# v through a staging buffer, a cast and SBUF copies of key windows, in a sliding-window attention with a feed-forward layer

## The chip, the cores and the metric

The kernel runs on one core of a Trainium2 chip. Times are device microseconds (us) of that core. "The time of a kernel" is the median of its runs; a comparison is a ratio, computed as the mean time of one kernel's fast runs over that of the other's fast runs of the same rounds, with a 95% interval. It is therefore not quite the ratio of the medians that are quoted beside it. A run that is over 1.5% slower than the fastest of the same kernel counts as slow and stays out of the ratio.

## The reference, cut to what matters

```python
# q, k, v: [8 batches, 8 heads, 576 positions, 64]
scores = q @ k.T / sqrt(64);  mask = |i - j| <= 32
x = (softmax(where(mask, scores, -1e9)) @ v)        # -> [4608 tokens, 512]
h = x @ w_in                                        # [4608, 2048]
out = elu(h) @ w_out                                # [4608, 512]
```

All inputs and the output are fp32 in HBM. The kernel computes in bf16.

## The kernel before

Attention works on blocks of 64 queries. A block needs the 128 keys around it, so v lies in SBUF as nine *windows* per batch, `vw[key in window, window, head, 64 + 1]`: 128 partitions, a row of 520 bf16 (1040 bytes) per key and window, with a column of ones that yields the softmax sum. Two blocks make a *pair* (128 tokens; 36 pairs). Four pairs make a *tile* (in before the first tile is cut into two of two pairs), for which the hidden layer (matmul with w_in, ELU) and the output layer are computed while the next tile's pairs go through attention.

```python
NVB = 3                                   # three sets of windows
def load_v(b):                            # even windows, cast by the DMA itself: runs of 64 elements
    vt = vw[b % NVB]; vb = v[b].rearrange("h s d -> s h d")
    nc.gpsimd.dma_start(out=vt[WIN:128, 0, :, 0:D], in_=vb[0:128 - WIN])
    for qb in range(2, NQB - 1, 2):
        nc.gpsimd.dma_start(out=vt[:, qb, :, 0:D], in_=vb[lo:lo + 128])
    ...
def shift_v(b):                           # odd windows: two copies on the SP queue
    nc.sync.dma_start(out=vt[0:QB, 1:NQB:2], in_=vt[QB:128, 0:NQB - 1:2])
    nc.sync.dma_start(out=vt[QB:128, 1:NQB:2], in_=vt[0:QB, 2:NQB:2])
def X(i): nc.sync.dma_start_transpose(dst, xs)     # xt <- xs, on the SP queue too
def OUT(t, c): nc.sync.dma_start(out[r:r + 128, :], y)
```

q and k come as fp32 in four loads per batch, issued by ACT from batch 1 on, into four staging buffers `stg`; POOL casts them to `bf`. A planner in the kernel puts all operations in an order by assumed durations; on the chip each engine then works in that fixed order. In the built programs the transfers issued by SP or ACT take eight completion semaphores in turn: all 116 of before do, and all 192 of after. The records of the two traces show the same eight, and in them no transfer is issued before the one that used its semaphore before, eight places earlier in the program, has landed, whichever of the two engines issued that one. In after 13 are issued within 0.02 to 0.18 us of that landing; the two waits examined below are among them. I call this *the line of eight*. The transfers issued by POOL have semaphores of their own in the traces, eight in before (48 transfers) and four in after (4).

The softmax here doesn't subtract the row's maximum and nothing guards it: scores larger than these inputs give would overflow.

Of the kernel before, what the change touches and what calls it, by code (L numbers as in the profile page):

```python
# [8 lines left out]
FP32 = mybir.dt.float32  # L9
BF16 = mybir.dt.bfloat16  # L10
AX = mybir.ActivationFunctionType
ALU = mybir.AluOpType
# [8 lines left out]
class Plan:  # L21
# [5 lines left out]

    def __init__(self):
        self.ops = {}

    def op(self, name, eng, dur, rank, deps, fn, dma=0.0, lag=0.0,
           at=0.0):


        self.ops[name] = (eng, dur, rank, tuple(deps), fn, dma, lag, at)

    def run(self):
        ops = self.ops
        done, users, left = {}, {}, {}
        for n, o in ops.items():  # L40
            left[n] = len(o[3])
            for d in o[3]:
                assert d in ops, (n, d)
                users.setdefault(d, []).append(n)
        free = {}
        server = 2.0
        ready = {}
        for n, o in ops.items():
            free.setdefault(o[0], 0.0)
            if left[n] == 0:  # L50
                ready.setdefault(o[0], {})[n] = 0.0
        order = []
        while len(order) < len(ops):
            best = None
            for e, rs in ready.items():
                if not rs:
                    continue
                t = max(free[e], min(rs.values()))
                n = min((ops[n][2], n) for n, r in rs.items() if r <= t)[1]
                if best is None or t < best[0]:  # L60
                    best = (t, e, n)
            t, e, n = best
            del ready[e][n]
            _, dur, _, _, fn, dma, lag, at = ops[n]
            free[e] = t + dur
            if dma:
                server = max(server, t + dur) + dma
                end = server + 2.0
            else:
                end = t + dur + lag  # L70
            end = max(end, at)
            done[n] = end
            order.append((t, n))
            for u in users.get(n, ()):
                left[u] -= 1
                if left[u] == 0:
                    ue = ops[u][0]
                    r = max(done[d] + (0.0 if ops[d][0] == ue
                                       and not (ops[d][5] or ops[d][6] or ops[d][7]) else self.LAT)
                            for d in ops[u][3])  # L80
                    ready.setdefault(ue, {})[u] = r
        self.done = done
        self.order = order
        for _, n in order:
            ops[n][4]()
# [3 lines left out]
def kernel(  # L89
# [47 lines left out]
    w_in_sb = const.tile([128, NDO, D_FF], BF16)  # L137
    w_out_sb = const.tile([128, NFO, DM], BF16)
    NKB = 2
    NVB = 3  # L140
    NPB = 2
    kT = [const.tile([128, HP, KW], BF16, name=f"kT{i}") for i in range(NKB)]
    qT = [const.tile([128, HP, S], BF16, name=f"qT{i}") for i in range(NKB)]
    vw = [const.tile([128, NQB, H, VW], BF16, name=f"vw{i}") for i in range(NVB)]
    pm = [const.tile([128, H, 3 * QB], BF16, name=f"pm{i}") for i in range(NPB)]

    live = {}
# [47 lines left out]
            nc.vector.tensor_copy(dst, src)  # L195


    def load_v(b):
        vt = vw[b % NVB]
        vb = v[b].rearrange("h s d -> s h d")  # L200
        nc.gpsimd.dma_start(out=vt[WIN:128, 0, :, 0:D], in_=vb[0:128 - WIN])
        for qb in range(2, NQB - 1, 2):
            lo = qb * QB - WIN
            nc.gpsimd.dma_start(out=vt[:, qb, :, 0:D], in_=vb[lo:lo + 128])  # L204
        lo = (NQB - 1) * QB - WIN
        nc.gpsimd.dma_start(out=vt[0:S - lo, NQB - 1, :, 0:D], in_=vb[lo:S])  # L206

    def shift_v(b):
        vt = vw[b % NVB]
        nc.sync.dma_start(out=vt[0:QB, 1:NQB:2], in_=vt[QB:128, 0:NQB - 1:2])  # L210
        nc.sync.dma_start(out=vt[QB:128, 1:NQB:2], in_=vt[0:QB, 2:NQB:2])


    def QK(i):
# [73 lines left out]

    def XE(i):
        dst, pt = live.pop(("XT", i))  # L290
        nc.vector.tensor_copy(dst, pt)


    gs, es, ys = {}, {}, {}
# [12 lines left out]
    def EX(t, fo):  # L307
# [2 lines left out]
        nc.scalar.activation(e, ps, AX.Exp)  # L310
        es[t, fo] = (ps, e)

    def FF(t, fo):
        ps, e = es[t, fo]
        f = ep.tile([128, ps.shape[1]], BF16, name="f", tag="f")
        nc.vector.tensor_scalar(f, e, -1.0, 0.0, ALU.add, ALU.min)  # L316
        es[t, fo] = (ps, f)

    def GG(t, fo):
        ps, f = es.pop((t, fo))  # L320
        nc.vector.tensor_tensor(gs[t][:, fo, :], ps, f, ALU.max)  # L321

    def ypool(t, c):
        if t < NT - 1:
# [21 lines left out]
        nc.sync.dma_start(out[r:r + 128, :], ys.pop((t, c)))  # L346


    sizes = [2, 2] + [4] * 8
    tiles, where = [], {}  # L350
    p0 = 0
    for t, n in enumerate(sizes):
# [10 lines left out]
    w_in_v = moe_w_in.rearrange("(o p) f -> p o f", p=128)  # L363
    w_out_v = moe_w_out.rearrange("(o p) f -> p o f", p=128)

    def WI(c):
        nc.gpsimd.dma_start(out=w_in_sb[:, :, c * FC:(c + 1) * FC],
                            in_=w_in_v[:, :, c * FC:(c + 1) * FC])

    def WO(c):  # L370
        o = NFO // NWC
# [7 lines left out]
    def prank(i):  # L379
# [3 lines left out]
              ("k", 1): "POOL"}  # L383
    engs = {"DVE": nc.vector, "ACT": nc.scalar, "POOL": nc.gpsimd}
    cdur = {"DVE": 1.2, "ACT": 1.5, "POOL": 1.5}
    LAND = {(0, "k", 0): 6.2, (0, "q", 0): 8.2, (0, "k", 1): 10.5,
            (0, "q", 1): 13.0, (1, "k", 0): 27.0, (1, "q", 0): 31.0,
            (1, "k", 1): 35.0, (1, "q", 1): 39.0}
    for b in range(B):
        need = prank(b * NQB // 2)  # L390
        r0 = need - 60
        t0 = where[b * NQB // 2][0]
        early = [("H", max(t0 - 2, 0), 15 if t0 == 2 else 8)] if b > 1 else []
        for half in range(2):
            for nm in ("q", "k"):
                deps = list(early)
                if b == 1:
                    deps.append(("SM", 0))
                if b:
                    deps.append(("C", b - 1, nm, half))  # L400
                P.op(("L", b, nm, half), "ACT" if b else "SP", 0.1,
                     r0 + half, deps,
                     lambda b=b, nm=nm, half=half: load_qk(
                         b, nm, half, nc.scalar if b else nc.sync),
                     dma=0.0 if b < 2 else 2.2, lag=2.0,
                     at=LAND.get((b, nm, half), 0.0))
                eng = casts0[nm, half] if b == 0 else "POOL"
                deps = [("L", b, nm, half)]
                if b >= 2:
                    deps += [("T", b - 2, nm, hp) for hp in range(HP)]  # L410
                P.op(("C", b, nm, half), eng, cdur[eng], need - 30 + half, deps,
                     lambda b=b, nm=nm, half=half, eng=eng:
                     cast(b, nm, half, engs[eng]))
        deps = list(early)
        if b > 1:
            deps += [("WO", c) for c in range(NWC)]
        if b >= NVB:
            last = ((b - NVB + 1) * NQB - 1) // 2
            deps = [("AV", last, 0), ("AV", last, 1)]
        if b == 1:  # L420
            deps.append(("C", 0, "k", 1))
        P.op(("LV", b), "POOL", 4.5, (-2000, -899)[b] if b < 2 else r0, deps, lambda b=b: load_v(b),
             dma=5.0 if b > 1 else 0.0, at=(17.0, 45.0)[b] if b < 2 else 0.0)
        P.op(("SV", b), "SP", 0.2, need - 20, [("LV", b)],
             lambda b=b: shift_v(b), lag=4.5)
        for hp in range(HP):
            for nm in ("q", "k"):
                n = hp * 2 + (nm == "k")
# [13 lines left out]
                     lambda b=b, nm=nm, hp=hp: E(b, nm, hp))  # L442

    for c in range(NWC):
        P.op(("WI", c), "POOL", 1.0, -990 + c,
             [("C", 0, "k", 1)], lambda c=c: WI(c),
             at=(19.5, 24.0, 28.5, 33.0)[c])
        P.op(("WO", c), "POOL", 1.0, -890 + c, [("C", 1, "q", 1)],
             lambda c=c: WO(c),
             at=(50.0, 54.0, 58.0, 62.0)[c])  # L450

    for i in range(NPAIR):
        r = prank(i)
# [13 lines left out]
        P.op(("MK", i), "DVE", 0.85, r, deps, lambda i=i: MK(i))  # L467
        t, c = where[i]
        for g in range(2):
            deps = [("MK", i)] + [("SV", b) for b in bs]  # L470
            if i < NC0:
                if i:
                    deps.append(("RN", i - 1, g))
# [14 lines left out]
        if i < NC0:  # L488
            if i:
                deps.append(("X", i - 1))  # L490
            P.op(("XT", i), "PE", 0.3, r + 3, deps, lambda i=i: X(i))
            P.op(("X", i), "DVE", 0.42, r + 3, [("XT", i)],
                 lambda i=i: XE(i))
        else:
            P.op(("X", i), "SP", 1.2, r + 3, deps, lambda i=i: X(i), lag=4.0)

    hseq = [(t, fo) for t in range(NT) for fo in range(NFO)]
    for n, (t, fo) in enumerate(hseq):
        np_ = tiles[t][1]
        fr = np_ / 4  # L500
        r = PER * tiles[t][0] + 2 * fo * fr
        deps = [("X", tiles[t][0] + np_ - 1), ("WI", fo * NWC // NFO)]
        if n >= 3:
            deps.append(("GG",) + hseq[n - 3])
        if t >= 2:
# [4 lines left out]
        if n >= 3:  # L510
            deps.append(("FF",) + hseq[n - 3])
        P.op(("EX", t, fo), "ACT", 0.17 + 0.43 * fr, r, deps,
             lambda t=t, fo=fo: EX(t, fo))
        P.op(("FF", t, fo), "DVE", 0.1 + 0.33 * fr, r, [("EX", t, fo)],
             lambda t=t, fo=fo: FF(t, fo))
        P.op(("GG", t, fo), "DVE", 0.16 + 0.53 * fr, r, [("FF", t, fo)],
             lambda t=t, fo=fo: GG(t, fo))
# [23 lines left out]
    with tc.manual_schedule():  # L541
# [17 lines left out]
            channel_multiplier=-1)  # L559
        nc.gpsimd.tensor_copy(masks, mf)  # L560
        for t in vw:
            nc.vector.memset(t[0:WIN, 0, :, 0:D], 0.0)
            nc.vector.memset(t[128 - WIN:128, NQB - 1, :, 0:D], 0.0)
            nc.vector.memset(t[:, 0:NQB:2, :, D:VW], 1.0)
        for t in kT:
            nc.vector.memset(t[:, :, 0:WIN], 0.0)
            nc.vector.memset(t[:, :, WIN + S:KW], 0.0)
        for t in pm:
            nc.vector.memset(t[:, :, QB:2 * QB], 0.0)
        P.run()  # L570
# [30 lines left out]
```

## Time and profile before

| | before |
|---|---|
| time | 367.35 us (three runs, 365.93 to 369.72) |
| profiled span | 364.8 us, granted clock 0.991 |
| PE busy | 314.2 us (86%) |
| transfers on SP and ACT / on POOL | 116 / 48 |
| DMA time by queue, sum of shares | 78.3% of 364.8 us = 286 us of all 16 engines |

PE is the engine that should set the time. It stands still for 50.6 us, most of them in the first 130. The lines that show this are in the prediction.

### The profile page before, as it was taken

How to read it: one execution, taken by the hardware profiler on the slowest of the kernel's cores; microseconds unless marked ns; L12 is line 12 of the kernel's file. 1: busy time of each engine (PE TensorE's matmuls, PEld its weight loads, DVE VectorE, ACT ScalarE, POOL GpSimd, SP SyncE). 2: the span in 40 equal slices, each digit the busy share in tenths (PEclk: the TensorE clock that was granted, in tenths of full speed). 3: DMA queues.
4: the chain of work that ended last, by engine and by line, in shares of the span. 5: the costliest groups of instructions: out<-in, count | busy, mean ns of one | idle time of the engine just before them, and what ended most of it. 6: DMA issues, size and time to landing. Idle time of an engine off the chain costs nothing.

```text
span 364.8 us, 7010 instructions
## 1 busy us (share of the span) xinstructions
PE 314.2 (86%) x2725; PEld 168.9 (46%) x2768; DVE 252.9 (69%) x565; ACT 177.2 (49%) x290; POOL 86.1 (24%) x93
## 2 busy tenths in 40 slices
PE   1415889669877999999999999989999999999995
PEld 1314666334434544554455445445554444444442
DVE  4216899475779499886887787778788778756610
ACT  3431477236453654754565466555654535443421
POOL 7623810490036004500540240033000000000000
PEclk9999999899999899999999999999999999999999
DMA  8999999999698639994995793195112121111012
GB/s 173 172 251 276 121 198 194 196 135 174 147 242 102 72 101 214 131 138 105 242 127 69 175 210 85 45 234 114 45 51 66 46 58 45 43 49 40 29 65 78
DMA packets 81504, 46.13 MB, mean 126 GB/s; under 512 B 56384, under 2 KB 76864, under 8 KB 81472
## 3 DMA queue, kind: packets, MB, share of 16 engines
q0 software_dynamic: 41728, 8.92, 33.4%
q1 hardware_dynamic: 28544, 20.26, 25.4%
q10 hardware_dynamic: 11200, 16.52, 19.0%
q8 instruction: 21, 0.34, 0.4%
q14 instruction: 11, 0.09, 0.1%
HBM read 36.70 MB, written 9.44 MB: 126 GB/s over the span
## 4 chain that ended last, share of the span: by engine, by line
PE 58%; DVE 18%; DMA 14%; issue 3%; ACTq 2%; POOL 2%; ACT 1%; SPq 1%; POOLq 0%; DVEq 0%
PE psY L335 24%; PE psH L302 24%; DMA vw<-vw 6%; DVE g L321 6%; DVE f L316 6%; DMA xt<-xs 5%; DVE pm L243 4%; PE psO L255 4%; DMA vw<-in_v_dram 3%; PE psT L180 2%; DVE xs L270 2%; ACTq L155 2%; PE psS L220 2%; PE psO L335 1%; PE psS L335 1%
## 5 line engine op out<-in xcount | busy, mean ns | idle before, releaser
L302 PE MATMUL psH<-xt,w_in_sb 128*128 128x512 bf16 (+1 forms) x624 | 147.3, 360 | 4.5 <-DVE g L321 2.4
L310 ACT ACTIVATE e<-psH 128x512 f32<-128x512 f32 (+1 forms) x160 | 88.1, 555 | 115.9 <-PE psH L302 90.1
L335 PE MATMUL psY<-w_out_sb,g 128*128 128x512 bf16 x501 | 131.8, 383 | 3.1 <-ACT y L341 1.1
L316 DVE TENSOR_SCALAR f<-e 128x512 bf16<-128x512 f32 (+1 forms) x160 | 75.7, 473 | 45.8 <-ACT e L310 45.7
L321 DVE TENSOR_TENSOR g<-psH,f 128x512 bf16<-128x512 f32 (+1 forms) x160 | 102.0, 637 | 5.1
L302 PEld LDWEIGHTS <-w_in_sb 128*128 128x128 bf16 x640 | 60.4, 99 | 61.2 <-issue 6.1
L335 PEld LDWEIGHTS <-g 128*128 128x128 bf16 x576 | 52.3, 98 | 55.0 <-issue 2.7
L170 POOL CAST bf<-stg 96x1536 bf16<-96x1536 f32 x29 | 43.5, 1501 | 107.1 <-DMA stg<-in_k_dram 89.1
L255 PE MATMUL psO<-vw,pm 128*128 128x65 bf16 x544 | 30.7, 198 | 17.9 <-DMA vw<-vw 8.3
L231 ACT ACTIVATE pu<-psS 128x1024 bf16<-128x1024 f32 x36 | 36.8, 1021 | 12.7 <-PE psS L220 10.3
L255 PEld LDWEIGHTS <-pm 128*128 128x128 bf16 x576 | 27.1, 102 | 30.9 <-issue 8.1
L243 DVE TENSOR_TENSOR pm<-pu,masks 128x512 bf16<-128x512 bf16 x72 | 34.0, 514 | 4.8 <-ACT pu L231 4.8
L180 PEld LDWEIGHTS <-bf 96*128 96x128 bf16 x384 | 23.7, 104 | 28.2 <-ACT bf L168 8.1
L270 DVE TENSOR_TENSOR xs<-psO,rc 128x256 bf16<-128x256 f32 x68 | 28.9, 424 | 5.5 <-DMA xt<-xs 3.2
L180 PE MATMUL psT<-ident,bf 96*128 96x96 bf16 x348 | 25.4, 211 | 7.0 <-POOL bf L170 3.6
L341 ACT COPY y<-psY 128x512 f32<-128x512 f32 x33 | 19.4, 586 | 19.4 <-PE psY L335 14.3
L268 DVE RECIPROCAL rc<-psO 128x4 f32<-128x4 f32 x68 | 12.1, 178 | 22.0 <-PE psO L255 21.5
L193 ACT COPY qT<-psT 128x576 bf16<-128x576 bf16 x30 | 19.1, 638 | 15.9 <-PE psT L180 15.9
L204 POOL DMA_DIRECT2D vw<-in_v_dram x24 | 21.3, 900 | 15.5 <-PE psO L255 15.3
L220 PE MATMUL psS<-qT,kT 64*128 64x64 bf16 x576 | 16.0, 196 | 3.6 <-ACT pu L231 3.2
L220 PEld LDWEIGHTS <-kT 64*128 64x128 bf16 x576 | 11.3, 98 | 15.3 <-issue 14.5
L206 POOL DMA_DIRECT2D vw<-in_v_dram x8 | 6.5, 812 | 41.4 <-PE psO L255 40.6
(42 smaller groups left out, 74.1 us busy)
## 6 DMA issues: line engine op xcount, KB each, us to landing
out_dram<-y SPq DMA_DIRECT2D x36, 256.0 KB, 2.1
stg<-in_k_dram ACTq DMA_DIRECT2D x14, 576.0 KB, 9.3
stg<-in_q_dram ACTq DMA_DIRECT2D x14, 576.0 KB, 10.9
vw<-vw SPq DMA_DIRECT2D x16, 260.0 KB, 8.5
vw<-in_v_dram POOLq DMA_DIRECT2D x24, 128.0 KB, 8.2
w_in_sb<-in_moe_w_in_dram POOLq DMA_DIRECT2D x4, 512.0 KB, 13.7
w_out_sb<-in_moe_w_out_dram POOLq DMA_DIRECT2D x4, 512.0 KB, 11.3
vw<-in_v_dram POOLq DMA_DIRECT2D x16, 96.0 KB, 11.4
```

The lines of the kernel that those rows point to most:

```text
L170: eng.tensor_copy(dst, src)
L180: nc.tensor.transpose(pt[:, j, :], src[:, j, 2 * hp:2 * hp + 2, :], ident[0:PR, 0:PR])
L220: nc.tensor.matmul(psS[:, h % 2, s, hp, :], lhsT=kT[b % NKB][base:base + 64, hp, qb * QB:qb * QB + 128], rhs=qT[b % NKB][base:base + 64, h ...
L231: nc.scalar.activation(pu, live.pop(("S", i)), AX.Exp, scale=SCALE)
L243: nc.vector.tensor_mul(dst, pu[:, :, s], mb)
L255: nc.tensor.matmul(o[:, j, :], lhsT=p[:, h, s * QB:s * QB + 128], rhs=vw[b % NVB][:, qb, h, :], start=(s == 0), stop=(s == 1))
L270: nc.vector.tensor_mul(live["X", i][:, g * HP:(g + 1) * HP, :], o[:, :, 0:D], rb)
L302: nc.tensor.matmul(ps, lhsT=w_in_sb[:, do, fo * 128:(fo + 1) * 128], rhs=xts[t][:, do, :], start=(do == 0), stop=(do == NDO - 1))
L310: nc.scalar.activation(e, ps, AX.Exp)
L316: nc.vector.tensor_scalar(f, e, -1.0, 0.0, ALU.add, ALU.min)
L321: nc.vector.tensor_tensor(gs[t][:, fo, :], ps, f, ALU.max)
L335: nc.tensor.matmul(ps, lhsT=gs[t][:, fo, c * 128:(c + 1) * 128], rhs=w_out_sb[:, fo, :], start=(fo == 0), stop=(fo == NFO - 1))
```

## The change

The intent: v comes in long runs by hardware queues in place of 36,864 runs of 64 elements issued by POOL, is cast by POOL and then copied on chip into the windows. w_in likewise comes as fp32 and is cast on chip. All tiles get four pairs, and ACT takes some of the work of DVE in the first two tiles.

```diff
-    NVB = 3
+    NVB = 2
+    vbf = const.tile([VP, VT, H, VW], BF16)          # VP = 72 partitions, VT = 8 keys in each
-    def load_v(b): ...                                # 5 DMAs on POOL per batch
-    def shift_v(b): ...                               # 2 copies on SP per batch
+    def load_v(b, half, eng):                         # 2 loads per batch, ACT's queue from batch 1 on
+        t = stg.tile([VP, HP, VT * D], FP32, name="stg", tag="stg")
+        eng.dma_start(out=t, in_=v[b, half * HP:(half + 1) * HP].rearrange(
+            "h (p t) d -> p h (t d)", t=VT))          # runs of 2 KB
+    def cast_v(b, half, eng): ...                     # vbf <- stg
+    def window(b, qb):                                # 9 copies on SP per batch
+        nc.sync.dma_start(
+            out=vw[b % NVB][r:r + hi - lo, qb].rearrange("k h d -> k (h d)"),
+            in_=vbf[lo // VT:hi // VT].rearrange("p t h d -> p t (h d)"))
     ...
-        nc.vector.tensor_copy(dst, pt)                # xt of the first four pairs
+        nc.scalar.copy(dst, pt)
+            nc.scalar.activation(f, e, AX.Relu, bias=1.0, scale=-1.0)   # every 2nd block, tiles 0 and 1
-    sizes = [2, 2] + [4] * 8
+    sizes = [4] * 9
-    def WI(c): nc.gpsimd.dma_start(out=w_in_sb[...], in_=w_in_v[...])
+    def WL(c): nc.scalar.dma_start(out=wst[n][:, c % 2], in_=w_in_v[...])   # fp32, into g's buffers
+    def WI(c, half): ...                              # casts on POOL and ACT
     ...
```

A window copy reads 128 rows of 1040 bytes from 16 partitions, eight rows in each, and writes them to 128 partitions. With it there are 192 transfers (72 of them window copies) and 4 on POOL.

## The prediction

> **What bounds the kernel now.** I read the page's slices first, then the chain of waits, then windows of 10 us, then the PE timeline for the moments at which work starts.
>
> ```profile
> PE   1415889669877999999999999989999999999995
> DVE  4216899475779499886887787778788778756610
> PEclk9999999899999899999999999999999999999999
> DMA  8999999999698639994995793195112121111012
> GB/s 173 172 251 276 121 198 194 196 135 174 147 242 102 72 101 214 131 138 105 242 127 69 175 210 85 45 234 114 45 51 66 46 58 45 43 49 40 29 65 78
> ```
>
> A slice is 9.12 us. From slice 14 on (about 130 us) PE is full; before that it has holes, and DMA is at 9 tenths in the first ten slices while it moves only 121 to 276 GB/s. So there are two stages: to about 85 us the transfers set the pace, afterwards PE does. The windows of 10 us say how much is lost: up to 130 us PE is busy 89.6 us, so 40.4 us idle; from 130 to 364.8 only about 10 us idle.
>
> ```profile
> 7.39 11.70 DMA vw<-in_v_dram
> 19.10 10.88 DMA vw<-vw
> ...
> 60.58 13.35 DMA xt<-xs
> ...
> 84.68 9.62 DMA vw<-vw
> ```
>
> The chain names the early waits: v's first load ends at 19 us, its shifted copy at 30 us, and only then can the first probability-times-v product (AV) start. Later xt (a transpose by DMA) and the second shifted copy take 13 and 10 us each, far over the 4.3 us that the issue table has as the median of such a transpose: they stand in a full DMA system.
>
> ```profile
> q0 software_dynamic: 41728, 8.92, 33.4%
> q10 hardware_dynamic: 11200, 16.52, 19.0%
> ...
> stg<-in_k_dram ACTq DMA_DIRECT2D x14, 576.0 KB, 9.3
> vw<-vw SPq DMA_DIRECT2D x16, 260.0 KB, 8.5
> w_in_sb<-in_moe_w_in_dram POOLq DMA_DIRECT2D x4, 512.0 KB, 13.7
> w_out_sb<-in_moe_w_out_dram POOLq DMA_DIRECT2D x4, 512.0 KB, 11.3
> ```
>
> The GpSimd queue takes a third of the DMA time with 41,728 packets. 36,864 of them (8 batches x 576 rows x 8 heads) are v in runs of 64 elements.
>
> ```profile
> L302 PE MATMUL psH<-xt,w_in_sb 128*128 128x512 bf16 x496 | 127.0, 379 | 2.6 <-DVE g L321 1.4 <-DMA xt<-xs 0.4
> L302 PE MATMUL psH<-xt,w_in_sb 128*128 128x256 bf16 x128 | 20.3, 287 | 1.8 <-DVE g L321 1.1
> L170 POOL CAST bf<-stg 96x1536 bf16<-96x1536 f32 x29 | 43.5, 1501 | 107.1 <-DMA stg<-in_k_dram 89.1 <-DMA stg<-in_q_dram 18.0
> L204 POOL DMA_DIRECT2D vw<-in_v_dram x24 | 21.3, 900 | 15.5 <-PE psO L255 15.3
> ```
>
> [...] the cost in a full stream comes from the chain, where a group of four 512-wide ones takes 0.86 us, and of four 256-wide ones 0.60 us. There 8 AV take 0.24 us, 16 scores (QK) 0.34, 6 input transposes 0.26.
>
> ```profile
> 36.12 1.86 PE L302 MATMUL psH<-xt,w_in_sb 128*128 128x256 bf16 x8
> 83.76 1.89 PE L302 MATMUL psH<-xt,w_in_sb 128*128 128x512 bf16 x8
> ```
>
> These are the two marks that I use: the first hidden-layer matmul (36.1 us), and the first of pairs 4 to 7 (83.8 us), from which on it is a PE-bound stream. (A pair is 128 tokens; there are 36.)
>
> [...] the DMA view of the first 60 us shows 208 to 226 GB/s while v's short runs are in flight and 266 to 296 GB/s around 22 to 34 us, when w_in's 2 KB runs flow. [...] the 96x1536 cast takes 1501 ns on POOL and 1471 on ACT.
>
> **The change, part by part.**
>
> v: 40 loads issued by POOL (24 at 0.90 us, 16 at 0.81: 34 us) and 16 shifted copies go. In comes, per batch, two loads of 288 packets of 2 KB, two POOL casts of 2048 elements (1501 x 2048/1536 = 2.0 us each, an estimate by size), and nine copies of 1040-byte rows on the SP queue. POOL stays far from a bound: 15 such casts add 30 us and the DMA issues that go were 34 us, on an engine busy 24%. In DMA time 4608 short packets per batch become 576 + 1088 larger ones. q10's line gives 0.19 x 364.8 x 16/11200 = 99 ns for a packet of about 1.5 KB[...]. I do not count this as fewer busy DMA microseconds, but as a rate nearer to the 280 GB/s of long runs.
>
> Start: at 280 GB/s batch 0 (3.54 MB) is in by 2.5 + 12.6 = 15 us. Cast of the second half on DVE 1.3 us, two copies issued at 0.65 and some 3 us to land: first AV about 21 to 22 us, against 30.1 now. Then four pairs at the present step of about 2.3 us per pair (AV starts at 30.12 and 31.58, then DVE-bound): the first tile is complete at 31 to 32 us, if w_in (4.19 MB behind batch 0, 15 us more, so 30 us, and a cast of 1 us) is there too. The first hidden matmul comes at about 32, with four pairs ready and not two.
>
> w_in by HWDGE and cast on chip: 8 casts of 1024 elements at 1.0 us, four on POOL and four on ACT, early and beside transfers. No time of its own.
>
> One tile size: 32 groups of 256-wide matmuls at 0.60 become 16 at 0.86: 19.2 - 13.8 = 5.4 us of PE saved, inside a stage that does not run PE-bound, so it does not come out as such.
>
> ACT takes a Relu for every second block of the first two tiles, and the xt copies. In tile 0 ACT then has 16 exps (0.60), 8 Relus (about 0.60), 7 evacuations (0.64) and 7 load issues (about 0.6): 23 us, against DVE's 8 x 0.50 + 16 x 0.69 = 15 us. So tile 0 is ACT-bound, 32 to about 54 us; DVE, which was at 90 to 95% between 40 and 60 us, is relieved.
>
> The hinge is the start of tile 1's hidden layer, mark two. In the built order there lie between the end of tile 0 and that mark on PE: 13 groups of the output layer (11.2 us), 8 input transposes (2.1), 7 QK (2.4), 11 AV (about 3): 18.7 us, so 54 + 18.7 = 73 us at the earliest. Two transfers speak too. The output groups need all of w_out before the second AV half of pair 5; batch 0, w_in, batch 1 and w_out are 15.5 MB, which takes until 58 us at 280 GB/s, and 66 if batch 2's q and k (2.36 MB) cut in; then PE still has 13 us. That makes 71 to 79. And pair 9 needs batch 2's v: 19 MB, 70 us, plus casts and copies, 77. I take 75.
>
> From there to the end, PE counts: 130 output groups and 128 hidden groups at 0.864 = 222.9; 27 pairs at 0.34 + 2 x 0.24 = 22.1; 40 transposes at 0.26 = 10.4. Sum 255.5 us. The same count for the kernel before from 83.76 us (135 + 128 groups, 28 pairs, 43 transposes) is 262, and it took 281, so 19 us were lost in the stream, some 9 of them between 84 and 130 us while transfers were still behind. With these mostly gone I take 12. So the span is 75 + 255.5 + 12 = 342.5 us, and the time 345 (the median lies 2.5 us over the profiled span).
>
> The landing times that are written in the code for the scheduler are a check. In before they give 27, 31, 35 and 39 us for batch 1, and the casts really start at 27.8, 31.5, 36.4 and 39.4. The new ones have batch 0's v by 15.5, w_in by 27, batch 1 by 40.5 and w_out by 58: my figures without the cut-in.
>
> **Rivals.** (a) The copies become the new wait: nine in a row take 5.9 us to issue on SP, where xt transposes and outputs stand in line behind them, and one v buffer must be copied out before the next cast. Against: seen from the steady stage, they are issued most of a batch (about 40 us) ahead. If it happened at each of 8 batches with 2 us, the time would be about 360. (b) ACT as bound: six load issues per batch instead of four, each 0.3 to 1.3 us in the chain, stop the exps. ACT is at 49% over the span, so only lumps count: some 5 us more, 350. (c) The early stage is bound by bytes alone: the same 36.7 MB are read. Then mark two stays near 84 and only the smaller work left there helps: 84 + 255.5 + 15 + 2.5 = 357. Against this: 121 to 200 GB/s in slices in which DMA is at 9 tenths. (d) Better: w_out in by 58 and no lump in the stream: 71 + 255.5 + 7 + 2.5 = 336.
>
> **Range and chances.** (d) and (c) span 336 to 357, and my centre is 345; I put the 8-in-10 range at 335 to 357. Faster by 2% means under 360.0 us, which all but (a) in full or a mixture of (a) and (c) gives: 0.92. Within 2%: 0.07. Slower needs a steady-state loss that I find no reason for: 0.01.
>
> **What would show it.** First AV near 22 and first hidden matmul near 32 us; GB/s of 250 and more in slices 1 to 5; GpSimd's queue below 5,000 packets[...]; mark two at 71 to 79; a PE at 9 tenths from slice 9 on. I am wrong if AV still waits for copies into vw beyond batch 2, if mark two is after 84, or if the stream after it loses 20 us or more.

75 us to mark two, 255.5 of counted PE time and 12 of loss make 342.5 us of span, and 2.5 more make the 345. 280 GB/s is the mean rate of before from 22 to 34 us, and 0.65 and 3 us for a copy are close to the mean issue and the shortest landing of before's shifted copies (0.64 and 3.1).

## The result, and the profile after

The changed kernel takes 414.95 us (four runs, 412.24 to 420.23) against 367.93 us of the kernel before beside it (365.93 to 369.72). The ratio is 1.1255 (1.1148 to 1.1362): 47 us slower. Its profiled run took 420.23 us and counts as slow (1.9% above the fastest of its kernel); the other three are fast. All four have a granted clock of 0.943 to 0.958. What is read from this trace below is far larger than the 2% in question.

The slices of the changed kernel (one is 10.46 us), to be set against those in the prediction:

```profile
PE   1302781969798794999885988899559999999996
...
PEclk9999996888899896999997999999959999999999
DMA  8999489957619649567985499569924622120102
GB/s 181 247 323 237 101 201 196 265 125 95 117 47 214 133 110 265 136 139 122 219 142 93 93 237 190 103 124 244 164 48 76 110 65 52 38 64 25 52 36 90
```

PE now has holes up to slice 30 (314 us), not only up to 130 us, and DMA stays busy as long. The rate in slices 2 to 4 is about as hoped (247, 323, 237; predicted 250 and more), and falls to 101 straight after. The queues, with packets, MB and share of the DMA time:

```profile
q1 hardware_dynamic: 34584, 26.23, 31.8%
q10 hardware_dynamic: 17512, 28.97, 29.2%
q0 software_dynamic: 2112, 2.10, 3.3%
```

GpSimd's queue is down to 2,112 packets, as predicted. In sum 64.8% of 418.5 us, 271 us, are a little *less* DMA time than the 286 before, though with the copies 57.7 MB move in place of 46.1. So the sum of DMA time does not explain the slower kernel. Such a sum is not occupancy: packets of several queues overlap, and in the first 83.8 us of before their times add up to 1.49 times what 16 engines have. The window copies (time that one holds SP in ns, least, median and most; first and last start in us):

```profile
L225 SPq DMA_DIRECT2D vw<-vbf x72: 544/822/1384, 24.1 to 327.2; - x72
```

The second mark of the prediction:

```profile
111.55 1.86 PE L318 MATMUL psH<-xt,w_in_sb 128*128 128x512 bf16 x4 [2.72 <-issue]
```

The first hidden matmul of all is at 50.5 in this timeline (predicted 32; 36.1 before), this first one of pairs 4 to 7 at 111.6 (predicted 75; 83.8 before). The stretch from there to the end, first of before and then of after (start:end and length, then busy time of PE, PEld, DVE, ACT, POOL, the clock, DMA share and GB/s):

```profile
83.76:364.80 281.04, 265.30 (x2133) 133.85 (x2169) 203.34 (x424) 141.92 (x226) 42.74 (x35) 0.99 0.57 107
```

```profile
111.55:418.50 306.95, 268.34 (x2057) 132.63 (x2096) 199.04 (x409) 142.02 (x229) 49.58 (x30) 0.95 0.56 117
```

So some 28 us are lost before mark two and 26 us after it, where PE stands for 38.6 us (306.95 - 268.34) in place of 15.7. Long pieces of the chain of waits (start, length, what):

```profile
14.30 19.88 DMA g<-in_moe_w_in_dram
...
62.31 8.88 issue
...
214.65 10.26 DMA xt<-xs
...
293.36 14.58 DMA xt<-xs
```

The last two are transposes that stand among a batch's loads. The first piece is a wait for w_in; ACT's evacuations of batch 0 stand behind a load of batch 1 meanwhile (the releaser that the second line names is only the last of several; the load waits in the line for the last w_in load, landed at 34.2):

```profile
34.28 0.35 ACTq L163 DMA_DIRECT2D stg<-in_k_dram  x1
...
35.29 0.64 ACT L201 COPY qT<-psT 128x576 bf16<-128x576 bf16 x1 [23.27 <-POOL w_in_sb L407]
```

The piece that is called "issue" is worth a look, since that word says only that the profile shows no wait. ACT's timeline there (start, length, instruction; idle time before it in brackets):

```profile
61.70 0.61 ACT L326 ACTIVATE e<-psH 128x512 f32<-128x512 f32 x1
71.19 0.32 ACTq L163 DMA_DIRECT2D stg<-in_k_dram  x1
71.61 0.63 ACT L336 ACTIVATE f<-e 128x512 bf16<-128x512 f32 x1 [9.30 <-issue]
```

ACT has ELU work to do, but the next instruction in its order is a load of k for batch 2. In the built program that load waits for the semaphore of a window copy of batch 1, eight places earlier in the line and issued by SP (in the trace it is issued at 63.04 and lands at 71.12). Until the copy lands, ACT does nothing, PE runs out of free hidden-layer buffers and stands too, and its next matmuls take 1.86 us for four in place of 0.86: PEclk falls to 0.6 in this slice.

```profile
73.01 1.86 PE L318 MATMUL psH<-xt,w_in_sb 128*128 128x512 bf16 x4 [9.29 <-DVE g L344]
```

The trace shows the half rate: after this gap of 9.29 us the granted clock is 0.50 until 77.2 us. The line of mark two above has the same 1.86 us, with a clock of 0.50, after a gap of only 2.72 us. That such a gap lowers the clock, and how long it must be, was not shown. In all PE is busy for 10.5 us more than before (324.7 against 314.2) although fewer matmuls are recorded (2,657 against 2,725).

### The profile page after: what moved, and what is told of

It reads as the page before. It is cut to its first block, busy times and chain, and to the rows that moved or that the text cites. A ratio compares the mean times of both kernels' runs of the same rounds, so it can differ in the third digit from the quotient of the medians.

```text
span 418.5 us, 6878 instructions
## 1 busy us (share of the span) xinstructions
PE 324.7 (78%) x2657; PEld 166.5 (40%) x2704; DVE 246.3 (59%) x510; ACT 188.8 (45%) x298; POOL 82.7 (20%) x68
## 3 DMA queue, kind: packets, MB, share of 16 engines
q0 software_dynamic: 2112, 2.10, 3.3%
## 4 chain that ended last, share of the span: by engine, by line
PE 55%; DMA 19%; DVE 11%; issue 6%; ACT 3%; ACTq 3%; POOL 1%; SPq 1%; POOLq 0%
PE psH L318 24%; PE psY L361 21%; DMA xt<-xs 8%; DMA g<-in_moe_w_in_dram 5%; DMA stg<-in_q_dram 5%; DVE pm L259 4%; ACTq L163 3%; PE psO L271 3%; PE psT L188 3%; DVE f L338 2%; DVE xs L286 2%; DVE g L347 2%; PE psS L236 2%; DMA stg<-in_v_dram 1%; PE psO L361 1%
## 5 line engine op out<-in xcount | busy, mean ns | idle before, releaser
L318 PE MATMUL psH<-xt,w_in_sb 128*128 128x512 bf16 x557 | 153.1, 403 | 34.3 <-DMA xt<-xs 15.0
L326 ACT ACTIVATE e<-psH 128x512 f32<-128x512 f32 x144 | 85.5, 597 | 141.7 <-PE psH L318 106.1
L338 DVE TENSOR_SCALAR f<-e 128x512 bf16<-128x512 f32 x128 | 65.7, 513 | 81.5 <-ACT e L326 81.3
L318 PEld LDWEIGHTS <-w_in_sb 128*128 128x128 bf16 x576 | 56.3, 102 | 100.5 <-issue 40.5
L347 DVE TENSOR_TENSOR g<-psH,f 128x512 bf16<-128x512 f32 x128 | 88.5, 691 | 4.4
L259 DVE TENSOR_TENSOR pm<-pu,masks 128x512 bf16<-128x512 bf16 x72 | 38.6, 577 | 17.7 <-ACT pu L247 17.5
L247 ACT ACTIVATE pu<-psS 128x1024 bf16<-128x1024 f32 x36 | 36.8, 1023 | 9.8 <-PE psS L236 9.1
L220 POOL CAST vbf<-stg 72x2048 bf16<-72x2048 f32 x15 | 29.0, 1932 | 56.9 <-DMA stg<-in_v_dram 50.0
L271 PE MATMUL psO<-vw,pm 128*128 128x65 bf16 x544 | 30.1, 198 | 9.5 <-DVE xs L286 5.2
L201 ACT COPY qT<-psT 128x576 bf16<-128x576 bf16 x30 | 19.1, 636 | 26.4 <-POOL w_in_sb L407 23.3
L344 DVE SCALAR_TENSOR_TENSOR g<-f,psH 128x512 bf16<-128x512 bf16 x16 | 10.9, 684 | 15.1 <-ACT f L336 15.1
## 6 DMA issues: line engine op xcount, KB each, us to landing
vw<-vbf SPq DMA_DIRECT2D x16, 97.5 KB
```

Of the source, the lines that this page charges most:

```text
L247: nc.scalar.activation(pu, live.pop(("S", i)), AX.Exp, scale=SCALE)
L259: nc.vector.tensor_mul(dst, pu[:, :, s], mb)
L271: nc.tensor.matmul(o[:, j, :], lhsT=p[:, h, s * QB:s * QB + 128], rhs=vw[b % NVB][:, qb, h, :], start=(s == 0), stop=(s == 1))
L318: nc.tensor.matmul(ps, lhsT=w_in_sb[:, do, fo * 128:(fo + 1) * 128], rhs=xts[t][:, do, :], start=(do == 0), stop=(do == NDO - 1))
L326: nc.scalar.activation(e, ps, AX.Exp)
L338: nc.vector.tensor_scalar(f, e, -1.0, 0.0, ALU.add, ALU.min)
```

## The experiments

Eighteen kernels were run, in five rounds, each beside the kernel before on the same chip. To compare starts, I read from each trace the time at which ACT begins the first exponent of pairs 4 to 7 (1 to 2 us after mark two); "rest" is the span from there.

| run | what it is | time, us | ratio to before (95%) | start | rest |
|---|---|---|---|---|---|
| before | | 367.9 | 1 | 84.8 | 280.0 |
| after | | 415.0 | 1.126 (1.115-1.136) | 113.4 | 305.1 |
| e1_win_pool | after, w_in loads on POOL | 411.2 | 1.126 (1.117-1.135) | 116.2 | 292.2 |
| e2_loads_pool | after, q, k, v loads on POOL | 430.4 | 1.172 (1.165-1.179) | 115.5 | 311.6 |
| e3_v_old | after, v as before | 372.6 | 1.014 (1.007-1.022) | 93.1 | 275.5 |
| e4_win_old | after, w_in as before | 403.0 | 1.083 (1.073-1.092) | 106.4* | 299.1* |
| f1_lead | after, loads a tile earlier | 412.3 | 1.123 (1.110-1.137) | 114.1 | 298.4 |
| f3_own_free | after, own staging for v, no gate | 423.4 | 1.153 (1.140-1.166) | 118.2 | 299.3 |
| e7_win_copies_pool | after, copies on POOL | 396.1 | 1.077 (1.062-1.091) | 107.1 | 287.6 |
| g5_replanned | after, reordered | 401.8 | 1.098 (1.090-1.106) | 107.4 | 293.8 |
| g1_no_copies | after, no copies from batch 2 on | 394.1 | 1.073 (1.065-1.081) | 111.0 | 282.1 |
| g2_no_v_loads | after, no v loads from batch 2 on | 391.2 | 1.067 (1.060-1.074) | 110.2 | 276.7 |
| i2_after_three_straight | after, 3 straight copies per batch | 390.2 | 1.051 (1.044-1.058) | 106.2* | 285.0* |
| f5_before_late_v | before, v late, two window sets | 368.0 | 1.005 (0.996-1.014) | 80.2 | 284.1 |
| h3_sizes_act | before, new tile size and ACT work | 369.3 | 1.006 (0.997-1.014) | 88.2 | 279.4 |
| g4_before_plus_copies | before + 72 scattered copies | 410.8 | 1.122 (1.116-1.128) | 97.5 | 312.1 |
| g8_before_copies_pool | the same on POOL | 415.6 | 1.128 (1.118-1.137) | 96.2 | 319.7 |
| i1_before_straight_copies | before + 72 straight copies | 382.4 | 1.042 (1.035-1.050) | 94.2 | 290.2 |
| g6_before_few_copies | before + 16 large straight copies | 382.7 | 1.045 (1.037-1.052) | 83.0 | 298.8 |
| g7_before_small_copies | before + 72 copies of 16 rows | 377.4 | 1.031 (1.025-1.037) | 93.1 | 283.2 |

(* profiled run slow. The medians of i2 and e4 mix two slow runs with two fast ones: 385.11 and 387.46 in i2, 395.15 and 398.76 in e4. Starts and rests are of single traces.)

A *scattered* copy reads eight rows from each of 16 partitions, as the new copies do; a *straight* one reads each row from another partition. The planner's entry of a changed operation changes with it. The letters of the theories are set anew in the expectations of each round.

### Round one: which part of the change?

My first theory was (A): the engines' fixed order and the line of eight; ACT and SP stand behind transfers that cannot be issued yet. Its rivals were (B) too many bytes or packets, (C) loads are slow when POOL issues them, (D) the tile size and ACT's new work.

```diff
 # e1_win_pool
-        nc.scalar.dma_start(out=wst[n][:, c % 2], in_=w_in_v[...])
+        nc.gpsimd.dma_start(out=wst[n][:, c % 2], in_=w_in_v[...])
 # e2_loads_pool
-                     b, half, nc.scalar if b else nc.sync),
+                     b, half, nc.gpsimd if b else nc.sync),
 # e3_v_old: load_v, shift_v and NVB = 3 of before, everything else of after
 # e4_win_old: WI of before (cast by the DMA, POOL), everything else of after
```

> The changed kernel, with the four fp32 loads of w_in issued by POOL instead of ACT; same bytes, same runs, same casts. Theory A (a DMA issued by SP or ACT stands until the DMA eight places earlier in the program, on either of the two, has landed, and everything behind it on that engine stands too): ACT no longer stands from 12 to 34 us, the first hidden matmul comes at 36 to 40 us instead of 50.5, the time falls from 414 to 395 to 403 us; the stops later in the stream stay. Rival B (bytes: [...]more SBUF traffic, w_in lands when it lands): first hidden matmul stays at 48 or later, time 408 or more.

> The changed kernel, with all loads of q, k and v from batch 1 on issued by POOL instead of ACT; w_in still by ACT. Theory A: ACT carries no wait on a transfer any more after the first microseconds and the copies on SP no longer stand behind loads, so the start and most of the later stops go: 360 to 385 us. Rival B: the same bytes move in the same runs, so the transposes still land late and the time stays above 400 us. Rival C (POOL-issued loads are slow to be issued[...]): as B, with POOL idle before its casts longer than now.

> The changed kernel with the v path of the kernel before (cast by DMA from POOL in short runs, shifted copies on SP); w_in, the one tile size and the ACT work as changed. Theory A: 72 copies and 16 loads leave the shared line of completions, the later stops go, some of the start stop stays: 370 to 390 us. Rival B with v as its cause: 360 to 375. Rival D (the one tile size or the work moved to ACT is the cause): stays above 400.

> The changed kernel with w_in loaded as before (cast by DMA from POOL straight into its place); v and the one tile size as changed. Theory A: only the start stop goes, as in the run with the w_in loads on POOL: 393 to 403 us, 10 or more below the changed kernel, the later stops stay. Rival B with v as its cause: within 5 us of the changed kernel (410 or more). Rival D: no change.

e3 gives back nearly everything: v's path is the cause, and what else changed costs 1.4%. e1 and e2 refute A in the form in which I had put it. In e1 the first softmax exponent ends at 19.1 us in place of 38.6, yet mark two comes no earlier. In e2 loads and casts stand in one order on POOL, and a wait for a transpose in the chain lasts up to 17.5 us. That e2 came out worse also spoke for C, and B was still possible. e4 gained 3.8%.

### Round two: has v lost its run-ahead?

A table of landings, made from the semaphore records of the traces, suggested a new theory, G. In before the windows of batch 4 are complete at 97 us and used at 165. In after those of batches 3 to 7 are complete within 5 us of the first exponent of that batch's pairs, before or after it: batch 3 needs 46 us from its first load (124.2) to its last copy (170.7). So v has no lead any more, as there are two window sets in place of three and its loads wait with those of q and k.

```diff
 # f1_lead
-  early = [("H", max(t0 - 2, 0), 2 if b == 2 else 8)] if b > 1 else []
+  early = ([("H", 0, 2)] if b == 2 else [("H", t0 - 3, 8)]) if b > 1 else []
 # f3_own_free: one staging buffer of v's own; v's loads wait for the cast of the half before
+  svp = ctx.enter_context(tc.tile_pool(name="svp", bufs=1))
-  t = stg.tile([VP, HP, VT * D], FP32, name="stg", tag="stg")
+  t = svp.tile([VP, HP, VT * D], FP32, name="sv", tag="sv")
 # f5_before_late_v (from before)
-    NVB = 3
+    NVB = 2
-            deps = [("AV", last, 0), ("AV", last, 1)]      # v's gate
+            deps += [("AV", last, 0), ("AV", last, 1)]     # the gate of q and k as well
 # e7_win_copies_pool
-        nc.sync.dma_start(out=vw[...], in_=vbf[...])
+        nc.gpsimd.dma_start(out=vw[...], in_=vbf[...])
```

> After's kernel with one edit: from batch 3 on, the six loads of a batch may be issued one tile earlier (gate: hidden block 8 of tile t0-3 in place of t0-2). Theory G (run-ahead): in the changed kernel a batch needs about 46 us from its first load to its last window copy (batch 3: 124 to 171 us), the gate gives it about 31 to 40, and before had v in place a batch or more ahead. G expects the stream after mark two to fall from 307 to about 275-280 us and the time to 375-390 us. Theory B (too many DMA bytes or packets in flight) and theory A (order of issue on SP and ACT) expect 400-415: the same transfers in the same queues.

> After's kernel with a staging buffer of v's own (one half of v; q and k keep four), and v's loads of batch 2 on no longer gated with q and k: they go as soon as the half before is cast. Same bytes, same copies, same engines. Theory G expects v's window copies to land well before the pairs need them and the time to be 375-395 us, with q and k of batch 2 no longer waiting for v's casts (mark two below 105 us). Theories A and B expect 400-415.

> The kernel before, with only v's run-ahead taken away: two window buffers in place of three, and v's loads gated by the same hidden block as q and k. Theory G expects a loss, 370-385 us: v's copies then land just in time or late. Theories A and B expect no change, 364-369 us: the transfers are those of before.

> After's kernel with all 72 window copies issued by GpSimd in place of SP. This takes 72 of 192 transfers out of the line of eight completion semaphores that SP and ACT share, and out of SP's order. Theory A (order and the line of eight) expects below 390 us. Theory G expects 400-415: the chain from load to copy stays as long.

G fell in all three runs. A tile more of lead changes nothing that can be told from noise, although the lead was really gained (by the semaphore records of f1 the windows of batches 4 to 7 were complete 22 to 39 us before the first exponent of their pairs), a staging buffer of its own makes it worse, and the kernel before does not mind losing its run-ahead. That the windows came just in time was a symptom. The one edit that helped, e7, touched the copies themselves; it gained less than A expected.

### Round three: take away, add, reorder

```diff
 # g1_no_copies (wrong result on purpose): window() only for b < 2
 # g2_no_v_loads (wrong result on purpose): loads and casts of v only for b < 2
 # g4_before_plus_copies (from before): a scratch tile that nobody reads
+  def window(b, qb):
+      nc.sync.dma_start(
+          out=scr[r:r + hi - lo, qb].rearrange("k h d -> k (h d)"),
+          in_=vw[b % NVB][0:(hi - lo) // 8, 1:9].rearrange("p t h d -> p t (h d)"))
 # g5_replanned: only the planner's assumed durations, e.g.
-            P.op(("W", b, w), "SP", 0.65, ..., lag=3.0)
+            P.op(("W", b, w), "SP", 1.02, ..., lag=6.0)
```

> Wrong result on purpose: after's kernel without the 54 window copies of batches 2 to 7 (AV reads the windows of batches 0 and 1 again); v is still loaded and cast. Theory C (the copies cost: SP's order, the line of eight semaphores, or their DMA time) expects 370-388 us. Theory L (v's loads through the four staging buffers of q and k hold up the loads) expects 400-415.

> Wrong result on purpose: after's kernel without v's 12 loads and 12 casts of batches 2 to 7; the 54 window copies stay (of the old v), released by the cast of q's second half of the same batch. Theory C expects 395-412 us, theory L 370-388.

> The kernel before with 72 extra copies on SP of the form of the new ones (16 partitions by 8 rows of 1040 bytes, spread over 128 partitions) into a scratch tile that nobody reads, released by v's shifted copies and by the AV of two batches before. Theory C expects 380-400 us although no arithmetic waits for them; theory L expects 364-372.

> After's kernel with only the assumed times that order the instructions replaced by those that its trace shows (loads, w_in and w_out by their measured landings; a window copy 1.02 us to issue and 6 to land in place of 0.65 and 3). Same instructions, another order on each engine. Theory P (each engine runs in an order made for landings that come 10 to 20 us later than assumed) expects 375-390 us; theories C and L expect 400-418.

g4 is the run that turned the study. 72 copies of the new form, added to the kernel before, cost 12.2%, as much as the whole change, though no arithmetic waits for their data. g1 points the same way from the other side, but neither g1 (394.1) nor g2 (391.2) fell in the range of either theory: each was between the two. Both bring the rest back to 277 to 282 us. So by these single traces the copies and v's loads hurt in the stream of the changed kernel only together. g5 missed its mark: a better order gains 2.4% (1.098 over 1.126), so part of the loss is that the order was made for landings that came later than assumed, but not most of it.

### Rounds four and five: number, bytes or form?

The copies could cost by their number (places in the line of eight), by their rows and bytes (DMA time), or by their form (eight rows from each of 16 partitions).

```diff
 # g6_before_few_copies: two per batch, straight
+  nc.sync.dma_start(out=scr[:, odd:NQB:2], in_=vw[b % NVB][:, odd:NQB:2])
 # g7_before_small_copies: nine per batch, 16 rows each
+  out=scr[8 * qb:8 * qb + 16, qb]...,  in_=vw[b % NVB][0:2, 1:9]...
 # g8_before_copies_pool: the copies of g4 issued by nc.gpsimd
 # i1_before_straight_copies: nine per batch, each row from its own partition
+  nc.sync.dma_start(out=scr[0:hi - lo, qb], in_=vw[b % NVB][0:hi - lo, qb])
 # i2_after_three_straight (wrong result on purpose): after, with vbf on 128 partitions and
+  nc.sync.dma_start(out=vw[b % NVB][:, WG[g]], in_=vbf[:, WG[g]])     # WG: even, odd, last
 # h3_sizes_act: before with sizes = [4] * 9, the Relus and the xt copies on ACT
```

> The kernel before with the bytes of the 72 extra copies in 16: two per batch on SP, together 1152 rows of 1040 bytes into the scratch tile (72 copies: 1088 rows per batch), released in the same way. Theory A (number: each copy takes a place in the line of eight completion semaphores, where a load or a transpose of SP or ACT waits for the one eight places earlier) expects 366-378 us. Theory B (DMA time of the rows) expects 395-410, as with 72 copies.

> The kernel before with 72 extra copies on SP of 16 rows each in place of 128: the number stays, rows and bytes fall to an eighth. Theory A expects most of the loss to stay, 385-405 us (less if a copy that lands sooner frees its place sooner); theory B expects 366-373.

> The kernel before with the 72 full extra copies issued by GpSimd in place of SP: rows, bytes and number stay, but they take no place in the line that SP and ACT share and none in SP's order. Theory A expects 366-380 us, theory B 395-410.

> The kernel before with the same 72 extra copies on SP, 1088 rows of 1040 bytes per batch, but each row is read from its own partition (128 source partitions) and not eight rows from each of 16. In the 16-partition form a packet of the copies took some 121 ns (from the DMA time that 72 of them add: 65.7 us times 16 engines over 8704 packets), in the form of two big straight copies 62 ns. Theory F (the form[...]) expects packets near 62-70 ns, the stream near 298 us as with the few copies, the start near 93 as with the small ones, and 388-396 us in all. If the form is nothing and the number and the bytes multiply, 405-412 us.

> Wrong result on purpose: after's kernel with all loads, casts and waits of the new v path, but with three straight copies per batch (1152 rows of 1040 bytes, each to its own partition) in place of nine scattered ones. Theory A plus F (number at the start, DMA time of the scattered rows in the stream) expects 383-398 us with mark two below 105 us. A theory by which the chain from load over cast to copy is too long, whatever the copies cost, expects 405-418.

> The kernel before with only the one tile size and its work on ACT (Relu of every second block of the first two tiles, the four xt copies); v and w_in as before. The run with the old v path and the new w_in gave 372.6 us (1.0142) and began its first hidden block at 45 in place of 36 us. If that delay is the new w_in's, this one takes 360-366 us and beats both kernels; if it is the tile size's (four pairs before the first hidden block in place of two), it takes 368-374.

**Number.** g7 has all 72 copies, but an eighth of the rows. It loses 3.1%, and in the profiled span most of it at the start (+8.3 us there, +3.2 in the rest). g6 has as many bytes in 16 copies and loses nothing at the start. ACT's timeline tells why; first the kernel before, then g4:

```profile
18.16 0.38 ACTq L155 DMA_DIRECT2D stg<-in_k_dram  x1
...
19.92 0.84 ACTq L155 DMA_DIRECT2D stg<-in_q_dram  x1
```

```profile
18.10 0.39 ACTq L156 DMA_DIRECT2D stg<-in_k_dram  x1
35.21 0.32 ACTq L156 DMA_DIRECT2D stg<-in_q_dram  x1
35.64 1.99 ACTq L156 DMA_DIRECT2D stg<-in_k_dram  x1
39.88 0.34 ACTq L156 DMA_DIRECT2D stg<-in_q_dram  x1
40.26 1.02 ACT L241 ACTIVATE pu<-psS 128x1024 bf16<-128x1024 f32 x1 [21.21 <-DMA scr<-vw]
```

Before, ACT issues batch 1's four loads within 2.6 us. In g4 the second one goes 17 us after the first, and the softmax exponent behind it in ACT's order comes 21 us late. The built program says what it waited for:

```
ACT  stg <- in_q_dram   waits for: semaphore 7 of the line, held by SP's scr <- vw
```

The same stop is there with small copies (g7: 17.46, then 33.16) and with straight ones (i1 lists an exponent that waited 20.3 us for `scr<-vw`). So the number works through the line and ACT's order, and it costs at the start, where loads are needed at once. In all, g6 and g7 both fell between the ranges of number and of DMA time: each is part of the cost.

**Rows and form.** i1 and g4 have the same number of copies and the same bytes, on the same queue; only the partitions that are read differ. The one loses 4.2%, the other 12.2%. The queue lines, of before, g4 and i1:

```profile
q1 hardware_dynamic: 28544, 20.26, 25.4%
```

```profile
q1 hardware_dynamic: 38336, 29.31, 39.1%
```

```profile
q1 hardware_dynamic: 38400, 29.32, 33.4%
```

A share times its span is DMA time of all 16 engines: 92.7 us before, 160.2 in g4 (0.391 x 409.6), 128.4 in i1 (0.334 x 384.4). The scattered copies added 67.5 us for 9,792 packets, 110 ns each (times 16 engines); the straight ones 35.7 us for 9,856, 58 ns each. (One packet in nine is a 4-byte one; for the 1040-byte rows alone the packet records give 121 and 63 ns.) Rows of the same 1040 bytes take nearly twice the time when 16 partitions are read. i1 came out 6 us better than its range. The lines of the scratch tile say the same (duration of the issue on SP in ns, then us from issue to landing), first g4, then i1:

```profile
L218 SPq DMA_DIRECT2D scr<-vw x72: 572/1158/3047, 26.5 to 284.4; - x72
...
DMA to landing us min/median/max: 3.8/6.9/13.3
```

```profile
L217 SPq DMA_DIRECT2D scr<-vw x72: 465/599/1608, 20.1 to 257.9; - x72
...
DMA to landing us min/median/max: 2.1/4.7/13.7
```

A scattered copy holds SP for 1158 ns in the median and lands after 6.9 us; a straight one for 599 ns and 4.7 us. Why rows from 16 partitions take longer was not shown: no run varied the partitions in steps.

In the "rest" column of the kernels made from before, the loss grows with the DMA time that the copies add: 7.4 us (g7) cost 3.2, 35.7 (i1) cost 10.2, 40.2 (g6) cost 18.8, 67.5 (g4) cost 32.1, from single traces. It is not in proportion: i1 and g6 add nearly the same and lose 10.2 and 18.8. Nor does the sum over all queues tell: e3 has more DMA time than before and after (85.4% of 368.7, 315 us), the largest part of it in POOL's queue, and takes 372.6 us. So it seems to matter in which queue the time is spent. g8, with the copies out of the line and of SP's order, loses as much as g4: its rest is even longer. It is not a clean test of the line, since on POOL each copy moves in packets of 4160 bytes that take 551 ns in the trace, 75 us of DMA time in all, and POOL, which issues v's loads too, waits before some of them; but here leaving the line saved nothing as long as the rows were read in this form. The early stop did go, as the line would have it: the first hidden matmul is at 35.3 us (36.1 before, 49.0 in g4), yet mark two comes 11 us late for a reason that was not followed.

**In the changed kernel.** i2 keeps all new loads, casts and waits, but copies in three straight pieces per batch. Its fast runs are at 1.051: 7.4 points of the 12.55 are gone. So what holds in the kernel before holds here too, and the theory of a chain that is too long whatever the copies cost misses: it expected 405 us and more.

**The rest of the change.** h3 cannot be told from before (1.006, 0.997 to 1.014), so no effect of tile size and ACT's work can be told from noise. With the new w_in as well (e3) it is 1.014. No version that I ran beats the kernel before.

## Why the prediction was wrong, point by point

The prediction was 345 us (335 to 357); the kernel takes 415.

- **"copies issued at 0.65 and some 3 us to land", "5.9 us to issue" for nine.** This is the term that failed. The nine copies of batch 0 took from 24.1 us to 36.8 from the first issue to the last landing, those of batch 1 from 61.5 to 79.2, those of batch 3 from 154.2 to 170.7: 13 to 18 us and not 9. SP's issues took 0.82 us in the median and not 0.65, with waits in the line between them, and the landings 4.5 us (by the semaphore records) and not 3. I had taken the issue time from a copy of another form: before's shifted copies read each row from another partition. The page of before had their landing too (8.5 us), and I did not use it.
- **"I do not count this as fewer busy DMA microseconds, but as a rate nearer to the 280 GB/s of long runs."** The bytes did move faster for 30 us. But I never priced the copies in DMA time: 8,704 packets at 95 ns (their mean in the packet records of after) are 52 us of all 16 engines, some 20 of them because of the form (57 ns in i2). v's new loads take 39 more (4,608 packets at 134 ns, the mean of 2 KB packets on ACT's queue). Before, v's short runs took 94.6 us and its shifted copies 20.5. So the sum fell by only a fifth, and the work moved from POOL's queue, which little else stood behind, into those in which loads, transposes and outputs stand.
- **"first AV about 21 to 22".** It was at 41.0. Batch 0's v landed at 22.8 us (15 predicted). By then 5.05 MB had moved, at 221 GB/s and not 280, and 1.51 MB of them were w_in's, which the prediction had put behind batch 0 and which came beside it. From 12 to 35.3 us ACT stood behind the first load of batch 1, which waits in the line for the last w_in load (landed at 34.2), and batch 0's evacuations stood behind it. e1 took this stop away, and the copies of batch 0 took its place (22.7 to 49.6).
- **Mark two at 75.** It followed at 111.6. e3 shows 93.1 with v's old path against 113.4, so about 20 of the 29 us lost there are v's.
- **"255.5 + 12" us from mark two on.** It was 307. PE's own count was close (268.3 us busy, of which some are at half clock); the 12 us of loss were 38.6. g1, g2 and i2 bring the rest to 277 to 285 us.
- **"Slower needs a steady-state loss that I find no reason for: 0.01."** The reason was rival (a), and I had set its price at 2 us for each of 8 batches, 360 us in all. Its mechanism was partly right (the copies are the new wait) and partly wrong: transposes did not suffer on the average. From issue to landing they took 5.1 us in the mean in after and 5.6 in before, by the semaphore records of the traces. What suffered first was ACT, which does not appear in rival (a), because SP's copies and ACT's loads share the line. Rival (b) had ACT's lumps from load issues at 5 us in all; one of them alone (62.3 to 71.2) was 8.9 us.
- **Readings of before's trace that were off.** The rates of 208 to 226 GB/s that the prediction puts down to v's short runs are those of q and k: v's short packets begin at about 12 us, and from 13.5 to 16.5 us, with them almost alone, the rate is 138 to 143. The direction is the same (266 to 296 with w_in's 2 KB runs). These rates count the cast loads by what they write (8.92 MB on POOL's queue, half of what is read), so the 121 to 200 GB/s that stand against rival (c) understate the reads. And one AV matmul ran at 22.4 us; the others waited for the copy until 30.1.
- **What was right.** POOL's cast of half a v took 1.9 us in the median (2.0 estimated); GpSimd's queue fell to 2,112 packets (below 5,000). It follows that neither of these was what mattered. (On v's loads the trace has only this: each gives 13 increments at its semaphore, where a load of q or k gives 16.)

**The account.** In points of the time before: 7.4 of 12.55 are the number and form of the copies (after to i2), 3.7 the rest of v's path (i2 to e3: loads and casts through the staging buffers that q and k use, and the copies that remain), 0.9 w_in's (e3 to h3, with intervals that overlap), 0.6 what is left, not distinguishable from nothing. The parts do not simply add: with v's new path w_in's old one was worth 3.8% (e4), with v's old path 0.9. What stays open: how the 7.4 points divide between number and form in the changed kernel itself (i2 changed both; in before the form alone was worth 8.0, i1 against g4); whether the form costs through the DMA time of its rows or through the time that it holds SP, since i1 against g4 changes both; and which part of the 3.7 is the form of v's loads, their bursts with q and k, or the straight copies.

## What to carry to other kernels

A transfer is to be priced by the DMA time of its packets and by what stands behind it in its queue and its line of semaphores, not by its bytes; here an on-chip copy that read eight rows from each of 16 partitions cost nearly twice as much DMA time per row as one that read each row from another partition (121 against 63 ns), and a load behind such copies in the line of eight was issued 17 us after the one before it (g4). When a new part is suspected, add it to the fast kernel with its result unused: that one run (g4) said more than all that had been taken from the slow one or altered in it until then. And data that arrive "just in time" in a trace need not be late for want of lead: more lead was worth nothing here (f1).
